# Attention, mixture of experts and SoLU on one core: the tokens of six experts turned on TensorE instead of by DMA

## The chip, the cores and the metric

One Trainium2 chip, one of its cores. The metric is the device time of the whole program in microseconds, lower is better. Every execution of a kernel gives one time; a profiled execution also gives the trace that the rows below are cut from.

Engines by the names of the profile: PE is TensorE (PEld its weight loads), DVE VectorE, ACT ScalarE, POOL GpSimd, SP SyncE, which here only issues DMAs.

## The reference, cut to what matters

```python
def reference(...):
    attn_out = _attn_ref(q, k, v, proj)              # hashed attention, 2 x 8 heads, 768 x 64
    x = attn_out.transpose(0, 2, 1, 3).reshape(1536, 512)
    x = _moe_ref(x, w_gate, w_output_gate, w1, w2)
    return _moe2_ref(x, w_in, w_out, g_ln)           # x @ w_in, SoLU, layer norm, @ w_out

def _moe_ref(x, w_gate, w_output_gate, w1, w2):      # w1 is 8 x 512 x 1024, w2 is 8 x 1024 x 512
    e_idx = np.argmax(x @ w_gate, axis=1)            # one expert for each token
    ...
    for e in range(8):
        mask = e_idx == e
        h = np.maximum(x[mask] @ w1[e], 0.0)
        ye = h @ w2[e]
        out[mask] = gate_w[mask, None] * eom[mask, e, None] * ye
```

Inputs and output are float32. The kernel works with pairs of f16 numbers, a high and a low part, and adds three f16 products for one float32 product.

## The kernel before

Three parts follow each other: attention (to about 264 us), the experts (264 to 416), and the SoLU layer (416 to the end). During attention every token's row, 512 high and 512 low f16 numbers, is scattered by POOL into a table `xs` in DRAM, where each expert has its own rows. The experts are then taken in an order that is computed on the chip from the counts, experts 0 and 1 first and the others by their counts, with a fixed number of columns for each place in the order: 224, 224, 224, 212, 200, 192, 184, 168.

An expert's work is two steps of four slots each. A slot of `m1` is 24 products (two blocks of 128 hidden units, four blocks of the 512 inputs, three f16 products each), with the tokens as the moving operand: `mm1` at lines 1107 to 1109, reading weights `wa` and tokens `xw`. A slot of `m2` is 24 products too: `mm2` at lines 1138 to 1140, reading `wb` and the hidden units `hh`. The list `slots` (lines 1163 to 1167) sets the order, 64 slots in all: m1 of 0, m1 of 1, and then m2 of e and m1 of e + 2 in turn, with m2 of 6 and 7 at the end. So m1 of expert 2 is slots 12 to 15, behind m2 of expert 0 in slots 8 to 11.

Products go to PSUM pool `ps_a`, four tiles of one bank. One slot of m1 fills one tile; ACT reads it twice (`ev1`, lines 1115 and 1117). Two slots of m2 fill one tile; ACT writes its high part to `yT` (`ev2`, L1147) and DVE the low part (L1148). L1148 is put into a list `late` and emitted in the next slot, behind that slot's other DVE work. Pool `ps_h`, two tiles of two banks, is not used in this part.

The weights come as float32 and are split on the way. For each piece of 128 x 1024 numbers, SP loads it into one of five `raw` buffers (`w_load`, L156 for w1, L158 for w2), ACT makes the high part (`w_hi`, L142), and DVE the low part one slot later (`w_lo`, L146), which frees the buffer. The list `prep` gives each slot from 4 to 47 and 52 to 55 one piece, loaded three slots ahead. Between them the SoLU weights are prepared too; they come as 64-bit numbers and need four DVE instructions and two of ACT (`wide_a`, `wide_b`, lines 122 to 131) before their own high and low parts. All this stands in the one loop over `slots` (from line 1209), and each engine works off its share in that order: in a slot ACT has its high part of a weight piece first and the evictions of the slot last.

The tokens: `x_load` (line 1035) takes the 224 rows of an expert out of `xs` by a transposing DMA into `xw`, 128 partitions by 8 blocks by 224 columns, with three buffers. SP issues it in the third slot of m1 of the expert two places earlier. Expert 0 has its tokens from another way.

Of the kernel before, what the change touches and what calls it, by code (L numbers as in the profile page):

```python
# [9 lines left out]
F16 = mybir.dt.float16  # L10
# [11 lines left out]
def kernel(  # L22
# [15 lines left out]
    nc = tc.nc  # L38
    B, H, S, D = q.shape
    NBIT = proj.shape[1]  # L40
    NT, DM = out.shape
    E, _, FF = w1.shape
# [5 lines left out]
    KD = DM // 128  # L48
    KF = FF // 128

    CAP = 224
# [16 lines left out]
    xs = dram.tile([E * NT, 2 * DM], F16, name="xs")  # L68
# [3 lines left out]
    ident16 = const.tile([128, 128], F16, name="ident16")  # L72
# [79 lines left out]
    def w_load(name, e, c):  # L152
        t = raw.tile([128, 1024], F32, tag="raw", name="raw")
        es = bass.ds(ids[e], 1) if e in ids else slice(e, e + 1)
        if name == "w1":
            nc.sync.dma_start(out=t, in_=w1[es, c * 128:(c + 1) * 128, :].rearrange("e p f -> (e p) f"))  # L156
        elif name == "w2":
            nc.sync.dma_start(out=t.rearrange("p (f d) -> p f d", f=2),  # L158
                              in_=w2[es, c * 256:(c + 1) * 256, :].rearrange("e (f p) d -> p (e f) d", p=128))
        elif name == "wi":  # L160
            nc.sync.dma_start(out=t, in_=w_in[c * 128:(c + 1) * 128, :])
        else:
            nc.sync.dma_start(out=t.rearrange("p (f d) -> p f d", f=2),
                              in_=w_out[c * 256:(c + 1) * 256, :].rearrange("(f p) d -> p f d", p=128))
        rawq[name, e, c] = t
# [760 lines left out]
    with tc.manual_schedule():  # L926
        with ExitStack() as es:
# [12 lines left out]
            for i in range(NU):  # L940
# [5 lines left out]
                jj, c = divmod(i - 8, 6)  # L946
# [78 lines left out]
        ps_h = ctx.enter_context(tc.tile_pool(name="ps_h", bufs=2, space=PSUM, reuse_waits="tile"))  # L1025

        moe = ExitStack()
        mp = moe.enter_context(tc.tile_pool(name="mp", bufs=2, reuse_waits="tile"))
# [1 line left out]
        for nm in ("wi", "wo"):  # L1030
            wt[nm, 0] = yp.tile([128, 2, 4096], F16, name=nm)
        yT = yp.tile([128, 2, KD, NT + CAP], F16, name="yT")
        xw_t, hh_t = {}, {}

        def x_load(e, r0, w=CAP):
            xw = mp.tile([128, 2 * KD, CAP], F16, tag="xw", name="xw", bufs=3)
            x = nc.sync.dma_start_transpose(out=xw[:, :, 0:w], in_=xs[r0, :])
            xw_t[e] = xw
            if e in (1, "x"):
                for y in scattered:  # L1040
                    tc.add_manual_dep(x.ins, y.name, mybir.DependencyInfo(
                        mybir.DependencyClass.Sync, mybir.DependencyReason.DATA), reason="rows of xs")

        def window():

            d = nc.vector
            nf, sf, done = (exp_f[:, x] for x in range(3))
            f, win_f = (mp.tile([1, x, y], F32, tag=nm, name=nm, bufs=1) for x, y, nm in ((8, E, "wf"), (1, 3, "wg")))
            m = mp.tile([1, 1], F32, tag="wm", name="wm", bufs=1)
            d.tensor_tensor(out=f[:, 0], in0=nf, in1=done, op=ALU.is_gt)  # L1050
            d.scalar_tensor_tensor(out=f[:, 0], in0=iota8[0:1], scalar=1.0, in1=f[:, 0], op0=ALU.add, op1=ALU.mult)
            d.tensor_reduce(out=m, in_=f[:, 0], op=ALU.max, axis=AX.X)
            d.tensor_tensor(out=f[:, 0], in0=f[:, 0], in1=m.to_broadcast([1, E]), op=ALU.is_equal)
            d.tensor_scalar(out=f[:, 1], in0=nf, scalar1=-float(WIN), scalar2=None, op0=ALU.add)
            d.tensor_tensor(out=f[:, 1], in0=f[:, 1], in1=done, op=ALU.min)
            d.tensor_tensor(out=f[:, 2], in0=f[:, 1], in1=row0[0:1], op=ALU.add)
            d.tensor_tensor(out=f[:, 3], in0=f[:, 1], in1=sf, op=ALU.add)
            d.tensor_copy(out=f[:, 4], in_=iota8[0:1])
            d.tensor_tensor(out=f[:, 5:8], in0=f[:, 2:5], in1=f[:, 0:1].to_broadcast([1, 3, E]), op=ALU.mult)
            d.tensor_reduce(out=win_f[:, 0], in_=f[:, 5:8], op=ALU.add, axis=AX.X)  # L1060
            d.tensor_copy(out=win[:, 0:3], in_=win_f[:, 0])
            d.scalar_tensor_tensor(out=done, in0=f[:, 0], scalar=float(WIN), in1=done, op0=ALU.mult, op1=ALU.add)
# [49 lines left out]
        def ev1(e, g, ps, n):  # L1112
            hh, ps = hh_t[e][..., 0:n], ps[..., 0:n]
            o = hh[:, 0, 2 * g:2 * g + 2]
            nc.scalar.activation(out=o, in_=ps, func=AF.Relu, scale=1.0 / 1024.0)
            hf = mp.tile([128, 2, CAP], F32, tag="hf", name="hf")[..., 0:n]
            nc.scalar.activation(out=hf, in_=ps, func=AF.Relu, scale=1.0 / 1024.0)  # L1117
            late.append(lambda: nc.gpsimd.tensor_tensor(out=hh[:, 1, 2 * g:2 * g + 2], in0=hf, in1=o,  # L1118
                                                        op=ALU.subtract))
# [4 lines left out]
        def run_late():  # L1124
            for f in late:
                f()
            late.clear()
# [14 lines left out]
        def ev2(e, g, start, n):  # L1142
            if g % 2 == 0:
                return
            hi, lo = (yT[:, a, g - 1:g + 1, bass.ds(start, n)] for a in range(2))
            py = psy[e][..., 0:n]
            nc.scalar.activation(out=hi, in_=py, func=AF.Copy, scale=1.0 / 1024.0)  # L1147
            late.append(lambda: nc.vector.scalar_tensor_tensor(out=lo, in0=py, scalar=1.0 / 1024.0, in1=hi,  # L1148
                                                               op0=ALU.mult, op1=ALU.subtract))
# [5 lines left out]
        def expert(e):  # L1155
            ids[e], rows[e] = (nc.values_load(slot_i[0:1, x, e:e + 1], engines=[ET.SP], min_val=0, max_val=mx,
                                              skip_runtime_bounds_check_because=why)
                               for x, mx in ((0, E - 1), (1, (E - 1) * NT)))
# [8 lines left out]
        slots = [(kd, e, g) for kd, e in seq for g in range(4)]  # L1167
# [6 lines left out]
        prep += [None] * 4 + [("w2", E - 1, c) for c in range(4)]  # L1174
        prep += [None] * (len(slots) - len(prep))

        LA = 3
        todo = {}
        placed = []

        def put(i, f, *a):
            todo.setdefault(i, []).append((f, a))

        def each(f, pc):
            for a in w_args(*pc):
                f(*a)
# [3 lines left out]
        for x in range(16):  # L1190
            i = WD[x] if wide else 3 + 3 * x
# [7 lines left out]
            elif x % 2 == 0:  # L1199
# [3 lines left out]
                put(i + 1, each, w_lo, pc)  # L1203
        for x in range(4, 4 + LA):
            if prep[x]:
# [3 lines left out]
        for i, (kd, e, g) in enumerate(slots):  # L1209
            if prep[i]:  # L1210
                each(w_hi, prep[i])
            if i and prep[i - 1]:
                each(w_lo, prep[i - 1])
            if 4 <= i < len(prep) - LA and prep[i + LA]:
                w_load(*prep[i + LA])
            if g == 1 and kd == "m1" and e + 3 < E:
                expert(e + 3)
            if g == 2 and kd == "m1" and e + 2 < E:
                x_load(e + 2, bass.ds(rows[e + 2], CAP))
            for f, a in todo.pop(i, []):  # L1220
                f(*a)
            run_late()
            if kd == "m1":
                ev1(e, g, mm1(e, g, CAPS[e]), CAPS[e])
            else:
                mm2(e, g, CAPS[e])
                ev2(e, g, starts[e], CAPS[e])
            if kd == "m2" and 4 * e + g < NTILE:
                t = 4 * e + g
                po = pos_all[:, t:t + 1]  # L1230
                nc.gpsimd.tensor_scalar(out=po, in0=slot_f[:, t:t + 1], scalar1=1.0, scalar2=1.0,
                                        op0=ALU.mult, op1=ALU.mult)
                x = nc.gpsimd.indirect_dma_start(
                    out=meta[:, :], out_offset=bass.IndirectOffsetOnAxis(ap=po, axis=0),
                    in_=me[:, t], in_offset=None).ins
                for y in placed:
                    tc.declare_no_dep(x, y, reason="every token has a row of its own")
                placed.append(x)
            if i == 30:
                mr = mp.tile([128, NTILE, 2], F32, tag="mr", name="mr", bufs=1)  # L1240
                nc.sync.dma_start(out=mr, in_=meta.rearrange("(t p) c -> p t c", p=128))
            if i == 36:
                nc.vector.tensor_copy(out=tok, in_=mr[:, :, 1])
                nc.vector.tensor_scalar(out=csc, in0=mr[:, :, 0], scalar1=float(2.0 ** -22), scalar2=None,
                                        op0=ALU.mult)
# [4 lines left out]
        mp = ctx.enter_context(tc.tile_pool(name="mq", bufs=2, reuse_waits="tile"))  # L1250
# [135 lines left out]
```

## Time and profile before

| | before |
|---|---|
| median of three runs | 554.01 us (552.87 to 557.27) |
| profiled execution, its own time | 556.92 us |
| span of that execution, first to last instruction | 555.1 us |
| mean granted clock of TensorE | 0.985 |
| busy share of PE, DVE, ACT, POOL | 93%, 71%, 62%, 46% |
| bytes moved by DMA | 83.13 MB, 150 GB/s on the mean |

Times in the rows are microseconds from the start of the span. A line such as L1107 is the line of the kernel that issued the instruction; `a<-xw,wa` are the tile written and the tiles read. An engine's idle time before an instruction stands in brackets with what ended it.

### The profile page before, as it was taken

The page shows a single profiled execution, that of the slowest core. Times are in us where ns is not written, and L with a number is a line of the kernel's source. Part 1 is how long each engine was busy: PE and PEld are TensorE (multiplying, and loading weights), DVE is VectorE, ACT ScalarE, POOL GpSimd, SP SyncE. Part 2 cuts the span into 40 slices and gives each one's busy share as a digit, 9 for nine tenths or more (in the row PEclk, how much of TensorE's full clock was granted, in tenths as well). Part 3 has the DMA queues.
Part 4 walks back from the last instruction along what each step waited for, and adds up shares of the span by engine and source line. Part 5 has one row for each costly group of instructions (what it writes and reads, how often), then busy time and mean ns, then how long its engine had stood idle before and what let it go on. Part 6 is the DMA issues. An engine that isn't in the chain of part 4 may idle for free. (4 is left out here: it accounts for less than half of the span.)

```text
span 555.1 us, 10812 instructions
## 1 busy us (share of the span) xinstructions
PE 518.3 (93%) x3900; PEld 351.5 (63%) x3900; DVE 395.9 (71%) x893; ACT 342.0 (62%) x642; POOL 257.7 (46%) x324
## 2 busy tenths in 40 slices
PE   6789999999999999999997989988999899999993
PEld 5446566666656655667996979987994344444441
DVE  7757777777777787766799987689995875645620
ACT  6677777877867777863386766587643453433420
POOL 7949493939696764716147546232220011121122
PEclk9999999999999999999998989998999999999998
DMA  5584977654839244304777999999600244243271
GB/s 170 109 222 105 225 151 221 151 155 103 230 82 222 90 92 132 91 1 170 234 219 144 330 225 262 235 341 342 243 3 2 43 85 100 58 89 83 57 113 58
DMA packets 107177, 83.13 MB, mean 150 GB/s; under 512 B 80624, under 2 KB 89456, under 8 KB 107120
## 3 DMA queue, kind: packets, MB, share of 16 engines
q1 hardware_dynamic: 104816, 76.09, 53.3%
q0 software_dynamic: 2304, 6.31, 3.2%
q8 instruction: 32, 0.52, 0.4%
q14 instruction: 25, 0.20, 0.1%
HBM read 51.43 MB, written 9.97 MB: 111 GB/s over the span
## 5 line engine op out<-in xcount | busy, mean ns | idle before, releaser
L566 ACT ACTIVATE p<-s,mx 128x768 f32<-128x768 f32 x96 | 95.2, 992 | 51.1 <-DVE mx L555 42.1
L551 DVE TENSOR_REDUCE mx<-s 128x1 f32<-128x768 f32 x96 | 91.7, 955 | 47.9 <-PE s L541 45.9
L580 PE MATMUL t<-ident,p 128*128 128x128 f32 x576 | 124.9, 274 | 0.7 <-ACT pt L582 0.7
L582 ACT COPY pt<-t 128x384 f32<-128x384 f32 x192 | 84.6, 478 | 10.8 <-PE t L580 9.5
L580 PEld LDWEIGHTS t<-ident,p 128*128 128x128 f32 x576 | 77.8, 141 | 15.3 <-ACT pt L582 5.0
L599 PE MATMUL v<-pt,v 128*64 128x384 f32 (+1 forms) x384 | 80.1, 503 | 0.9 <-DVE xt L626 0.9
L1118 POOL TENSOR_TENSOR hh<-hf,hh 128x448 f16<-128x448 f32 (+5 forms) x32 | 40.2, 1259 | 80.1 <-ACT hf L1117 80.1
L1262 PE MATMUL h<-wi,yT 128*128 128x512 f16 x288 | 65.8, 386 | 4.2 <-DVE so L1288 2.6
L1107 PE MATMUL a<-xw,wa 128*128 128x224 f16 (+5 forms) x224 | 57.3, 259 | 9.8 <-DVE yT L1148 8.8
L1138 PE MATMUL a<-hh,wb 128*128 128x224 f16 (+5 forms) x256 | 63.7, 252 | 0.0
L1139 PE MATMUL a<-hh,wb 128*128 128x224 f16 (+5 forms) x256 | 63.6, 251 | 0.0
L1140 PE MATMUL a<-hh,wb 128*128 128x224 f16 (+5 forms) x256 | 63.5, 251 | 0.0
L1329 PE MATMUL o<-wo,zT 128*128 128x512 f16 x288 | 63.5, 379 | 0.0
L541 PE MATMUL s<-k,q 128*128 128x384 f16 x192 | 58.3, 330 | 4.1 <-ACT p L566 4.1
L541 PE MATMUL s<-b,cm 128*128 128x384 f16 x192 | 57.2, 326 | 2.3 <-DVE b L510 1.1
L1109 PE MATMUL a<-xw,wa 128*128 128x224 f16 (+5 forms) x224 | 57.5, 260 | 1.4 <-DVE wa L146 1.4
L1108 PE MATMUL a<-xw,wa 128*128 128x224 f16 (+5 forms) x224 | 57.4, 259 | 0.0
L1262 PEld LDWEIGHTS <-yT 128*128 128x128 f16 x288 | 28.2, 99 | 40.3 <-DVE so L1288 3.8
L1329 PEld LDWEIGHTS <-zT 128*128 128x128 f16 x288 | 28.2, 98 | 34.0
L541 PEld LDWEIGHTS <-q 128*128 128x128 f16 x192 | 19.0, 99 | 39.7 <-issue 37.7
L1277 ACT ACTIVATE ex<-h,st,csc 128x1024 f32<-128x1024 f32 x12 | 14.4, 1203 | 43.3 <-DVE st L1300 32.6
L1301 POOL TENSOR_TENSOR st<-st,nhalf 128x2 f32<-128x2 f32 x12 | 8.5, 707 | 68.6 <-DVE st L1300 68.6
(255 smaller groups left out, 1017.7 us busy)
## 6 DMA issues: line engine op xcount, KB each, us to landing
raw<-in_moe_w_dram SPq DMA_DIRECT2D x64, 512.0 KB, 5.8
raww<-in_moe_w_in_dram SPq DMA_DIRECT2D x8, 512.0 KB
raww<-in_moe_w_out_dram SPq DMA_DIRECT2D x8, 512.0 KB, 6.9
xs<-raw SPq DMA_DIRECT2D x8, 448.0 KB
v<-in_v_dram SPq DMA_DIRECT2D x8, 384.0 KB
q<-in_q_dram SPq DMA_DIRECT2D x7, 384.0 KB, 3.8
k<-in_k_dram SPq DMA_DIRECT2D x7, 384.0 KB, 5.5
cm<-q SPq DMA_DIRECT2D x14, 96.0 KB, 2.1
```

The source lines that it names most:

```text
L541: nc.tensor.matmul(t[:, c, 0:SB], d[x, h][:, s], flat(d[y, h])[:, c * SB:(c + 1) * SB], start=first, stop=not first)
L551: nc.vector.tensor_reduce(out=mx[:, 0:1], in_=t[:, :, 0:SB], op=ALU.max, axis=AX.XY)
L566: nc.scalar.activation(out=p, in_=s_t.pop(i)[:, :, 0:SB], func=AF.Exp, scale=mx[:, 1:2], bias=mx[:, 2:3], accum_out=sums[j][:, qt, h:h + 1])
L580: nc.tensor.transpose(t[:, g * 128:(g + 1) * 128], p[:, c, g * 128:(g + 1) * 128], ident)
L582: nc.scalar.copy(out=pt[j, h][:, 3 * c:3 * c + 3, qt * 128:(qt + 1) * 128], in_=t[:, 0:SB].rearrange("p (g c) -> p g c", g=3))
L599: nc.tensor.matmul(pv[j, q0][64 * h:64 * h + 64, 0:w], vt[:, h, c], pt[j, h][:, c, q0 * 128:q1 * 128], start=(c == 0), stop=(c == NS - 1), ...
L1109: nc.tensor.matmul(ps[:, i, 0:n], w[:, 1, kk, fs], xw[:, kk], start=False, stop=(kk == KD - 1))
L1138: nc.tensor.matmul(ps, w[:, 0, f, ds], hh[:, 0, f], start=(f == 0), stop=False)
L1139: nc.tensor.matmul(ps, w[:, 0, f, ds], hh[:, 1, f], start=False, stop=False)
L1140: nc.tensor.matmul(ps, w[:, 1, f, ds], hh[:, 0, f], start=False, stop=(f == KF - 1))
L1262: nc.tensor.matmul(ps[:, c], yT[:, a, kk, ts], w_i[:, w, kk, c * 512:(c + 1) * 512], start=(kk == 0 and a == 0 and w == 0), stop=(kk == KD ...
L1329: nc.tensor.matmul(ps, zT[:, KF * a + f], w_o[:, w, f], start=(f == 0 and a == 0 and w == 0), stop=(f == KF - 1 and a == 1))
```

## The change

`x_load` keeps the transposing DMA for expert 1 and for the loop on overflowing tokens (`"x"`), which is not entered for these inputs. For experts 2 to 7 it loads rows: 112 partitions, two rows of 1024 f16 numbers on each, into a new tile `xr` with two buffers. A new function `x_turn` makes `xw` out of it: 16 transposes on TensorE (two halves of 512 inputs, four blocks of 128, two groups of 112 rows) into two tiles of `ps_h`, and two copies on ACT from PSUM into `xw`, which now has two buffers. `x_turn` is called in the slot before m1 of the expert, behind `run_late()` and ahead of that slot's own products.

```diff
         def x_load(e, r0, w=CAP):
-            xw = mp.tile([128, 2 * KD, CAP], F16, tag="xw", name="xw", bufs=3)
-            x = nc.sync.dma_start_transpose(out=xw[:, :, 0:w], in_=xs[r0, :])
-            xw_t[e] = xw
+            if e in (1, "x"):
+                xw = mp.tile([128, 2 * KD, CAP], F16, tag="xw", name="xw")
+                x = nc.sync.dma_start_transpose(out=xw[:, :, 0:w], in_=xs[r0, :])
+                xw_t[e] = xw
+            else:
+                xr = mp.tile([CAP // 2, 2, 2 * DM], F16, tag="xr", name="xr")
+                nc.sync.dma_start(out=xr, in_=xs[r0, :].rearrange("(r p) c -> p r c", r=2))
+                xr_t[e] = xr
...
+        def x_turn(e):
+
+            xr = xr_t.pop(e)
+            n = CAP // 2
+            xw = xw_t[e] = mp.tile([128, 2 * KD, CAP], F16, tag="xw", name="xw")
+            ps = [ps_h.tile([128, 2, 1024], F16, tag="h", name="xp")[:, 0] for b in range(2)]
+            for b in range(2):
+                for c in range(KD):
+                    for r in range(2):
+                        nc.tensor.transpose(ps[b][:, c * CAP + r * n:c * CAP + (r + 1) * n],
+                                            xr[:, r, (b * KD + c) * 128:(b * KD + c + 1) * 128], ident16[0:n, 0:n])
+            for b in range(2):
+                nc.scalar.copy(out=xw[:, b * KD:(b + 1) * KD], in_=ps[b][:, 0:KD * CAP].rearrange("p (c n) -> p c n", c=KD))
...
+        xr_at = [("m1", e, 0) for e in range(2, E)]
...
             run_late()
+            if i + 1 < len(slots) and slots[i + 1] in xr_at:
+                x_turn(slots[i + 1][1])
             if kd == "m1":
```

Lines behind `x_load` stand 19 or more lower in the changed kernel: L1107 becomes L1126, L1147 becomes L1166.

On ACT, in slots 10 and 11 (the third and fourth of m2 of expert 0), the order before is this, `wi` being a SoLU weight and `yT` the evictions of m2:

```order
L1147 ACTIVATE yT<-a 128x2x224 [waits PE_49]
L142 ACTIVATE wa<-raw 128x1024 [waits DMAHW7_49]
L142 ACTIVATE wi<-db 128x512 [waits DVE_49]
L142 ACTIVATE wa<-raw 128x1024 [waits DMAHW0_49]
L1147 ISA
L1147 ACTIVATE yT<-a 128x2x224 [waits PE_49]
```

and of the changed kernel, at the same place:

```order
L1166 ACTIVATE yT<-a 128x2x224 [waits PE_49]
L142 ACTIVATE wa<-raw 128x1024 [waits DMAHW7_49]
L142 ACTIVATE wi<-db 128x512 [waits DVE_49]
L142 ACTIVATE wa<-raw 128x1024 [waits DMAHW0_49]
L1061 COPY xw<-xp 128x896 [waits PE_49] x2
L1166 ISA
L1166 ACTIVATE yT<-a 128x2x224 [waits PE_49]
```

The two copies stand behind both weight conversions of the slots and ahead of the second eviction.

On PE, where m1 of expert 2 begins (behind the last product of slot 11), the order before:

```order
L1140 MATMUL a<-hh,wb 128x224
L1107 LDWEIGHTS wa [waits DMAHW2_49,PE_49]
L1107 MATMUL a<-xw,wa 128x224 [waits Activation_49]
L1108 LDWEIGHTS wa
L1108 MATMUL a<-xw,wa 128x224
```

and of the changed kernel:

```order
L1159 MATMUL a<-hh,wb 128x224
L1126 LDWEIGHTS wa
L1126 MATMUL a<-xw,wa 128x224 [waits Activation_49]
L1127 LDWEIGHTS wa
L1127 MATMUL a<-xw,wa 128x224 [waits Activation_49]
```

The wait for the transposing DMA is gone, and the second product waits for ACT as well: the first needs the first half of `xw`, the second the other. The 16 transposes stand 24 products earlier, at the head of slot 11, and the first of them waits for the row load.

On SP, where the tokens of expert 6 are loaded, the order before:

```order
L156 DMA raw<-in_moe_w_dram 128x1024 [waits DMAHW6_49,DVE_49]
L1037 ISA
L1037 DMA_TRANSPOSE xw<-xs 128x8x224 [waits DMAHW4_49,PE_49]
L1241 DMA mr<-meta 128x12x2 [waits DMASW7_49,Pool_49]
L156 ISA
```

and of the changed kernel:

```order
L156 DMA raw<-in_moe_w_dram 128x1024 [waits DMAHW6_49,DVE_49]
L1042 ISA
L1042 DMA xr<-xs 112x2x1024 [waits DMAHW4_49,PE_49]
L1263 DMA mr<-meta 128x12x2 [waits DMASW7_49]
L156 ISA
```

The row load stands where the transposing load stood.

## Rows read from the trace of the kernel before

**Rows 1.** The page: TensorE's busy time, and its clock in 40 slices.

```profile
PE 518.3 (93%) x3900; PEld 351.5 (63%) x3900; DVE 395.9 (71%) x893; ACT 342.0 (62%) x642; POOL 257.7 (46%) x324
...
PEclk9999999999999999999998989998999999999998
```

**Rows 2.** Busy time by stretch: PE, PEld, DVE, ACT, POOL, PEclk, DMA share, GB/s.

```profile
283.60:292.80 9.20, 9.20 (x99) 9.20 (x97) 9.13 (x9) 6.74 (x12) 4.63 (x4) 1.00 0.58 166
292.80:307.60 14.80, 11.28 (x99) 10.03 (x97) 14.73 (x17) 9.36 (x14) 9.90 (x11) 0.88 0.78 166
...
316.80:329.00 12.20, 10.07 (x98) 9.56 (x96) 9.90 (x13) 7.82 (x12) 6.45 (x7) 0.89 1.04 249
329.00:347.30 18.30, 18.07 (x195) 17.75 (x194) 14.65 (x15) 13.38 (x21) 11.00 (x13) 0.98 0.98 246
347.30:356.00 8.70, 8.70 (x99) 8.70 (x97) 6.60 (x5) 5.49 (x9) 3.28 (x3) 1.00 1.06 222
356.00:365.90 9.90, 8.10 (x99) 7.95 (x97) 5.89 (x9) 4.69 (x8) 0.22 (x1) 1.00 0.95 329
365.90:374.10 8.20, 8.20 (x99) 8.20 (x96) 7.80 (x9) 6.92 (x12) 4.68 (x4) 1.00 1.14 308
374.10:386.10 12.00, 9.48 (x99) 9.14 (x98) 11.93 (x14) 10.07 (x17) 2.88 (x3) 0.86 0.93 346
...
394.00:415.70 21.70, 21.69 (x291) 21.48 (x288) 20.36 (x28) 11.80 (x22) 5.01 (x4) 1.00 0.23 85
```

**Rows 3.** Waits of PE, 285 to 420 us: total, times, longest.

```profile
PE a L1107 <- DVE yT L1148: 8.8, 5, 2.5
```

**Rows 4.** Timeline of ACT in the expert part: start, duration, instruction, idle before.

```profile
299.55 0.63 ACT L142 ACTIVATE wi<-db 128x512 f16<-128x512 f32 x1 [1.76 <-DVE db L131]
...
301.03 0.53 ACT L1147 ACTIVATE yT<-a 128x448 f32 x1
...
318.87 0.53 ACT L1147 ACTIVATE yT<-a 128x448 f32 x1
...
338.06 1.06 ACT L142 ACTIVATE wa<-raw 128x1024 f16<-128x1024 f32 x1 [2.87 <-DMA raw<-in_moe_w_dram]
...
341.53 0.53 ACT L1147 ACTIVATE yT<-a 128x448 f32 x1
...
359.28 1.06 ACT L142 ACTIVATE wa<-raw 128x1024 f16<-128x1024 f32 x1 [3.23 <-DMA raw<-in_moe_w_dram]
...
361.97 0.50 ACT L1147 ACTIVATE yT<-a 128x424 f32 x1
...
380.71 0.48 ACT L1147 ACTIVATE yT<-a 128x400 f32 x1
...
396.92 0.48 ACT L1147 ACTIVATE yT<-a 128x384 f32 x1
```

**Rows 5.** Timeline of DVE near 360 us.

```profile
360.37 1.23 DVE L146 SCALAR_TENSOR_TENSOR wa<-raw,wa 128x1024 f16<-128x1024 f32 x1 [2.62 <-ACT wa L142]
```

**Rows 6.** SP: all transposing token loads (ns min/median/max), and its timeline from 347 us.

```profile
L1037 SPq DMA_TRANSPOSE xw<-xs x7: 1487/4407/5222, 265.9 to 366.6; - x7
...
347.60 4.41 SPq L1037 DMA_TRANSPOSE xw<-xs  x1
...
353.65 3.21 SPq L156 DMA_DIRECT2D raw<-in_moe_w_dram  x2
```

**Rows 7.** Stretches that DMA spent on a transposing load, and on weight rows.

```profile
312.00:314.00 2.00, 2.00 (x24) 2.00 (x22) 2.00 (x2) 1.51 (x3) 1.35 (x2) 1.00 1.26 246
338.00:340.00 2.00, 2.00 (x26) 2.00 (x24) 0.65 (x2) 1.74 (x2) 1.68 (x3) 1.00 1.03 410
```

**Rows 8.** f16 transposes on PE near the start: one group, and the durations in ns.

```profile
10.70 0.50 PE L378 MATMUL tp<-ident,kl 128*128 128x128 f16 x6
...
L378 PE MATMUL tp<-ident,kl x12: 219/219/243, 5.8 to 11.0; 128*64 128x128 f16 x6, 128*128 128x128 f16 x6
```

**Rows 9.** The nearest copy on ACT: f16 from PSUM, 768 columns.

```profile
L463 ACT COPY k<-tp x1: 805/805/805, 10.0 to 10.0; 128x768 f16<-128x768 f16 x1
```

More of the change, by code (lines that the diff above doesn't have):

```diff
@@ L1032 @@
         yT = yp.tile([128, 2, KD, NT + CAP], F16, name="yT")
-        xw_t, hh_t = {}, {}
+        xw_t, xr_t, hh_t = {}, {}, {}
         def x_load(e, r0, w=CAP):
-            xw = mp.tile([128, 2 * KD, CAP], F16, tag="xw", name="xw", bufs=3)
-            x = nc.sync.dma_start_transpose(out=xw[:, :, 0:w], in_=xs[r0, :])
-            xw_t[e] = xw
+            if e in (1, "x"):
[6 more added lines that the diff above has]
+                xr_t[e] = xr
             if e in (1, "x"):
```

## The prediction

> **What bounds the kernel now.** I began with the page: TensorE is busy for 93% of the span [rows 1], but the page says of a busy PE that it is not PE at its peak, so the question is where its instructions are spaced out. The change touches the expert stage alone. The view of busy time by stretch, cut at borders of slots, tells it [rows 2]. Four slots of 24 products with 224 columns take 9.2 us when nothing is late (283.6 to 292.8). The same work in 292.8 to 307.6 takes 14.8, so 5.6 us are lost there; 307.6 to 316.8 is again 9.2. With 212 columns four slots are 8.7 us, with 200 columns 8.2, so with 192 and 184 columns, in proportion, 7.9 and 7.6. By these, 316.8 to 329.0 loses 12.2 - 8.7 = 3.5 us, 329.0 to 347.3 loses 18.3 - 9.2 - 8.2 = 0.9, 356.0 to 365.9 loses 2.0 and 374.1 to 386.1 loses 4.4. After 307.6 that makes **10.8 us**, and nothing is lost after 394.
>
> The waits name the cause: PE at L1107 waits 8.8 us in 5 places for L1148 on VectorE [rows 3], the eviction that frees a PSUM tile of pool a. A second part is the clock: its mean is 0.88 in the 14.8 us from 292.8 [rows 2], that is some 3.5 us at 1.2 instead of 2.4 GHz behind such a wait, worth 1.7 us of work.
>
> Why L1148 is late stands in the timelines of ACT and DVE. Both prepare weights in program order, slot by slot, and run *behind* PE: in slot 11 (the fourth of m2 of expert 0) ACT first waits 1.76 us for DVE and gets to its last eviction at 301.03 [rows 4], though PE began the next slot at 292.8 [rows 2]. PE's four PSUM tiles let it run up to four slots ahead; that lead is what it uses up. After 320 the preparers are late again for another reason: ACT waits 2.87 and 3.23 us for weights from DMA [rows 4], and DVE then 2.62 for ACT [rows 5]. Ahead of the 3.23 stands a transposing load on SP at 347.60 that holds the queue 4.41 us; the next weight loads go out at 353.65 [rows 6].
>
> **The change, part by part.**
>
> *SP and DMA.* Six of the seven transposing loads become row loads. One transposing load holds SP 1.5 to 5.2 us, median 4.4; two weight loads beside it take 3.21 together with their waits, so at most 1.6 each [rows 6]. A weight load behind it thus goes out up to 4 us earlier. On the DMA engines, a stretch filled by a transposing load moves 246 GB/s, a stretch of weight rows 410 [rows 7]: for 448 KB that is 1.9 against 1.1 us, a gain of 0.8 us an expert. The Trainium skill says otherwise (Advanced Engine Details and Errata, § X-Bar Transpose (TRN2)): there transposing DMAs on this chip are as fast as regular ones. By that rule the DMA engines would gain nothing; rows 7 disagree on the rate, and the rule is silent on SP's time.
>
> *PE.* 16 small transposes are added in the slot before each of experts 2 to 7. The trace has a like row: six f16 transposes 128x128 in 0.50 us, one of them 0.22 long, so (0.50 - 0.22)/5 = 0.056 us each [rows 8]. 16 of them are 0.9 us (0.8 if 112 columns scale it down). The first set lies inside a stall (below), five are paid: **+4.5 us**.
>
> *ACT.* Two copies 128x896 from PSUM to f16 per expert. 128x768 takes 0.805 us [rows 9]; 896 columns scale to 0.94, and two in a row, overlapping a little, are 1.75. ACT is busy 9.36 of 14.8 us there [rows 2], so this is covered as work. It is not covered as a *place*: the copies stand in ACT's order behind the weight conversions of that slot, and the first product of the next expert on PE now waits for them. Queued behind PE's wait are all products of that expert; behind ACT's copies, the second eviction of the slot. Before, the tokens came by DMA, and no product needed ACT to be up to date so soon.
>
> *First border, m1 of expert 2.* ACT reaches the place of the copies at 301.03 [rows 4], and nothing before it changes: ACT waits there for DVE, and DVE is busy 9.13 of the 9.20 us before 292.8 and 14.73 of the 14.80 after it [rows 2]. So m1(2) starts at 301.03 + 1.75 = 302.8 instead of 292.8. Its four slots then run with all PSUM tiles free, but after a gap of 10 us I charge one drop of the clock (1.7): 302.8 + 9.2 + 1.7 = 313.7, against 307.6. **+6.1 us.**
>
> *From there on* PE is late enough that, if it never waits again, the starts are: m1(3) 313.7 + 9.2 + 0.9 = 323.8; m1(4) + 8.7 + 9.2 + 0.9 = 342.6; m1(5) + 8.2 + 8.7 + 0.9 = 360.4; m1(6) + 7.9 + 8.2 + 0.9 = 377.4; m1(7) + 7.6 + 7.9 + 0.9 = 393.8; end + 21.7 = 415.5, against 415.7. That is 6.1 + 4.5 - 10.8 = **-0.2 us**: the lead that PE had is spent in one piece at the first border, not in five.
>
> *The borders behind it.* PE now needs ACT up to date at each. Where ACT stood before, plus 1.75, is 320.6, 343.3, 363.7, 382.5 and 398.7 [rows 4]; against the starts above it is 3.2 early, then 0.7, 3.3, 5.1 and 4.9 late. If the preparers gain nothing, the largest of these, 5.1 us, is added. If each border gets back what it waited for behind a transposing load (2.87 of ACT for m1(4), 3.23 for m1(5) [rows 4], 2.62 of DVE for the last two [rows 5]), at most 2.5 is left, and 0 if the shorter waits around them go too. I take **1.5**, nearer to the low end, since the long waits are the ones that the removed loads head.
>
> What lies behind the stage (h, softmax, output) begins when PE ends it and only shifts. The sum on the profiled execution is 556.9 - 0.2 + 1.5 = 558.2 us (span 555.1 and 1.8 around it). That execution stands 2.9 above the median of the three runs, 554.0; on the median the same +1.3 gives **555.3 us**. The ends of the border term, 0 and 5.1, with one more drop of the clock at the upper, give 553.8 and 560.6.
>
> **The rivals.**
>
> 1. *The preparers gain nothing*: weight loads land as late as before because DMA is nearly full either way (share 0.95 to 1.14 in 347 to 374 [rows 2]). Then -0.2 + 5.1 = +4.9, and with a wait over 2 us and its drop of the clock +6.6: 558.9 to 560.6. For it speaks that DVE has no free time in 374 to 386 (11.93 of 12.00 [rows 2]). Against it, the two long ACT waits that follow transposing loads.
>
> 2. *Faster*: the first border costs nothing. This needs ACT to reach the copies by 291, ten us sooner than it did; then -0.2 - 6.1 = -6.3: 547.7. The place from which it decides is the conversion at 299.55 that waits for DVE [rows 4]; I see nothing in the change that speeds DVE up before it.
>
> 3. *The clock does not take transposes for work.* The 2.0 us lost in 356.0 to 365.9 left the clock at 1.00, the losses of 3.5 us and more did not [rows 2]; 0.9 us of transposes beside a wait of a us or so would then act as one longer gap at each of five borders, 1.7 us each: +1.3 + 8.5, 563.8. The Trainium skill has this rule (TensorE: Matmul & The Clock Gate, § Part 4: PE-mode transpose): transposes do not count as busy in the same way. The trace does not bear it out: through the attention part, where the transposes of L580 alternate with products, the clock row of the page shows full tenths [rows 1].
>
> 4. *The change does not do what it says*: the row loads come so late that the transposes wait. Each is issued 12 slots ahead of its use, some 25 us; I give it nothing of its own.
>
> **How the numbers follow.** Forecast as summed, 0.62; rival 1, 0.21; rival 2, 0.11; rival 3, 0.06. A measurement of this kernel can tell about 1% from no change, which is 5.5 us. Slower by more than that are half of rival 1, all of rival 3 and a tail of 0.04 of the forecast (two late weight loads at borders, each with its drop of the clock): 0.21. Faster is rival 2: 0.11. The rest, 0.68, is within 1%. The range leaves out the far half of rival 2 below and the far tail above: 550.5 to 562.5; the likeliest case alone spans 553.8 to 558.9.
>
> **What would show it.** Right: a gap on PE of about 10 us before m1 of expert 2 that ends on ACT's copy; after it m1(2) without waits for L1148; small waits for the copy, under 2 us, before m1(4) to m1(7); L1148 gone or nearly gone from PE's waits; SP's row loads under 1.6 us; the stage ending within 2 us of 415.7. Wrong: ACT at the copies by 295 (rival 2); waits of 3 us and more for the copy before m1(5) and m1(6) (rival 1); clock at its lower level after short waits (rival 3).

## The result, and the profile after

The changed kernel takes 560.5 us (median of 6 runs, 557.7 to 562.5) against 553.8 us (6 runs, 551.9 to 557.3): a ratio of **1.0127, 95% interval 1.0098 to 1.0156**, slower by about 1.3%. The forecast was 555.3 us, with a range of 550.5 to 562.5, and most of the chance on a difference within 1%. The time lies in the range, 5.2 us above the forecast, and the difference is over the 1% within which most of the chance lay.

The two profiled executions differ by less, 561.3 against 556.9 us: the expert stage begins 0.5 us later, is 5.1 us longer (264.5 to 421.3, 156.8 us, against 264.0 to 415.7, 151.7), and what lies behind it is 1.2 us shorter. The medians differ by more, 6.7 us, since the profiled execution before stands 3.1 us above its median and the changed one 0.8. What a profile can show is therefore the 5 us in the stage.

The page of the changed kernel, for [rows 1]: the clock row now has a 6 where there were an 8 and 9s.

```profile
PE 521.8 (93%) x3996; PEld 355.9 (64%) x3996; DVE 393.5 (70%) x893; ACT 353.4 (63%) x654; POOL 259.3 (46%) x324
...
PEclk9999999999999999999996999998999989999998
```

Busy time by stretch, changed kernel, for [rows 2]; the borders are now the first products of m1 of experts 2 (302.46), 3 (324.31), 4 (343.93), 5 (362.40), 6 (380.81) and 7 (399.50), and at 294.06 and 314.31 the ends of m2 of 0 and m1 of 2. Columns as there.

```profile
294.06:302.46 8.40, 0.15 (x3) 0.00 (x1) 8.33 (x12) 5.93 (x9) 6.71 (x8) 0.68 0.67 157
302.46:314.31 11.85, 11.39 (x96) 10.36 (x96) 8.42 (x10) 8.36 (x13) 3.06 (x3) 0.80 1.00 268
314.31:324.31 10.00, 10.00 (x115) 10.00 (x114) 9.22 (x9) 7.54 (x10) 8.84 (x8) 1.00 0.88 272
324.31:343.93 19.62, 18.87 (x211) 18.71 (x208) 16.74 (x17) 15.15 (x23) 14.58 (x15) 1.00 0.91 293
343.93:362.40 18.47, 17.91 (x209) 17.76 (x209) 13.57 (x14) 15.23 (x22) 4.08 (x4) 1.00 0.87 255
362.40:380.81 18.41, 17.11 (x210) 16.96 (x209) 17.33 (x21) 15.38 (x24) 5.04 (x4) 1.00 0.97 322
380.81:399.50 18.69, 18.12 (x208) 17.94 (x208) 14.64 (x19) 12.89 (x21) 4.56 (x4) 0.91 0.83 300
```

PE is idle for 8.3 us before m1 of expert 2 and runs at a mean clock of 0.80 behind that gap; later it loses 0.75 us before m1 of 4 (324 to 344), 0.56 inside it, 1.30 before m1 of 6, 0.57 inside it, and the mean clock is 0.91 from there to m1 of 7. The drop lies in one stretch, which has half the full clock:

```profile
382.40:385.90 3.50, 3.50 (x27) 3.47 (x25) 3.43 (x6) 1.77 (x4) 0.33 (x1) 0.51 0.84 291
```

PE's waits from 262 to 424 us (total, times, longest), for [rows 3]. The five waits for L1148 are gone; in their place stand waits for ACT's copy, L1061.

```profile
PE a L1126 <- ACT xw L1061: 10.3, 3, 8.3
PE a L1127 <- ACT xw L1061: 1.6, 3, 0.6
```

The timeline of ACT, changed kernel, for [rows 4]: the first border, and the border of m1 of expert 6 with what follows it.

```profile
300.04 0.63 ACT L142 ACTIVATE wi<-db 128x512 f16<-128x512 f32 x1 [1.76 <-DVE db L131]
...
301.52 1.69 ACT L1061 COPY xw<-xp 128x896 f16<-128x896 f16 x2
...
379.25 0.72 ACT L142 ACTIVATE wo<-db,g 128x512 f16<-128x512 f32 x1 [1.80 <-DVE db L131]
379.88 1.69 ACT L1061 COPY xw<-xp 128x896 f16<-128x896 f16 x2
...
384.64 0.48 ACT L1134 ACTIVATE hh<-a 128x368 f16<-128x368 f32 x1 [1.73 <-PE a L1128]
...
394.95 0.50 ACT L1166 ACTIVATE yT<-a 128x384 f32 x1 [2.16 <-PE a L1159]
```

The timeline of PE at the first border, m1 of expert 4 and m1 of expert 6, changed kernel, and below it the kernel before at m1 of expert 6.

```profile
302.46 0.35 PE L1126 MATMUL a<-xw,wa 128*128 128x224 f16 x1 [8.25 <-ACT xw L1061]
...
343.93 0.25 PE L1126 MATMUL a<-xw,wa 128*128 128x200 f16 x1 [0.75 <-ACT xw L1061]
...
380.81 0.24 PE L1126 MATMUL a<-xw,wa 128*128 128x184 f16 x1 [1.30 <-ACT xw L1061]
```

```profile
374.10 0.24 PE L1107 MATMUL a<-xw,wa 128*128 128x184 f16 x1
```

This pair is the core of the case. At m1 of expert 6 ACT stands nearly where it stood before: its copies begin at 379.88, and the eviction at the same place of the order began at 380.71 in [rows 4]. But before, PE had begun m1 of expert 6 at 374.10, 6.6 us ahead of ACT, and now it may begin only at 380.81, behind the first copy.

All waits of ACT from 308 to 416 us show the other half. Before, the first fence, ACT waits for DMA and for DVE, never for PE. After, the second fence, it hardly waits for DMA, less for DVE, and 17.3 us for PE's products (9.4 + 7.9).

```profile
ACT wo L142 <- DVE db L131: 16.8, 7, 3.7
ACT wb L142 <- DMA raw<-in_moe_w_dram: 10.7, 7, 3.2
ACT wa L142 <- DMA raw<-in_moe_w_dram: 7.7, 6, 3.2
```

```profile
ACT yT L1166 <- PE a L1159: 9.4, 8, 2.2
ACT hh L1134 <- PE a L1128: 7.9, 13, 3.0
ACT wo L142 <- DVE db L131: 6.1, 4, 2.9
ACT wa L142 <- DMA raw<-in_moe_w_dram: 2.5, 5, 1.1
```

So PE waits for ACT at a border, and ACT, done with the copies, then waits for PE to make something to evict.

SP, changed kernel, for [rows 6]: the row loads hold SP for 0.33 us each, and the pair of weight loads that went out at 353.65 now goes out at 350.18.

```profile
L1042 SPq DMA_DIRECT2D xr<-xs x6: 333/334/349, 273.6 to 365.9; - x6
```

```profile
350.18 3.74 SPq L156 DMA_DIRECT2D raw<-in_moe_w_dram  x2
```

The added work, changed kernel: a copy's duration (ns, min/median/max), for [rows 9], and the stretch that one set of 16 transposes takes on PE, for [rows 8].

```profile
L1061 ACT COPY xw<-xp x12: 886/906/911, 301.5 to 398.1; 128x896 f16<-128x896 f16 x12
```

```profile
290.95:291.74 0.79, 0.79 (x18) 0.79 (x17) 0.79 (x2) 0.79 (x3) 0.06 (x1) 1.00 0.80 270
```

### The profile page after: what moved, and what is told of

The parts are those of the page before. It is cut to its first block, busy times and chain, and to the rows that moved or that the text cites. A ratio compares the mean times of both kernels' runs of the same rounds, so it can differ in the third digit from the quotient of the medians.

```text
span 559.5 us, 11014 instructions
## 1 busy us (share of the span) xinstructions
PE 521.8 (93%) x3996; PEld 355.9 (64%) x3996; DVE 393.5 (70%) x893; ACT 353.4 (63%) x654; POOL 259.3 (46%) x324
## 5 line engine op out<-in xcount | busy, mean ns | idle before, releaser
L1126 PE MATMUL a<-xw,wa 128*128 128x224 f16 (+5 forms) x224 | 57.0, 258 | 11.3 <-ACT xw L1061 10.3
```

The lines of the kernel that those rows point to most:

```text
L1126: nc.tensor.matmul(ps[:, i, 0:n], w[:, 0, kk, fs], xw[:, kk], start=(kk == 0), stop=False)
```

## The experiments

Two questions: is it the added work, or the place of the copies in ACT's order; and if the place, which border? All ratios are to runs of the kernel before made beside the experiment (its medians there 556.5 to 556.7), each with its 95% interval.

**No wait for the copies.** All work stays, but no product needs it. The products of experts 2 to 7 read expert 1's tokens, which are given a buffer of their own so that they stay; the main line of the edit:

```diff
-            xw = xw_t[e][:, :, 0:n]
+            xw = xw_t[e if e in (0, "x") else 1][:, :, 0:n]
```

> The changed kernel, but the products of experts 2 to 7 read expert 1's tokens, which lie there since before the stage; the transposes and the copies are still made, and nothing reads the copies. Place theory (the loss is that PE waits for copies that stand late in ACT's order): the gap of 8.3 us before m1 of expert 2 and the waits of 1.3 and 1.9 us before m1 of experts 4 and 6 go, PE uses up its lead at L1148 again, and the time is 548 to 556 us, a ratio of 0.99 to 1.005. Work theory (the loss is the work that is added, 0.8 us of transposes on PE and 1.75 us of copies on ACT for each expert): the ratio stays at 1.010 to 1.013.

Measured: ratio 1.0007 (0.9982 to 1.0032). The largest row of PE's waits in it, 275 to 424 us:

```profile
PE a L1126 <- DVE yT L1167: 7.6, 4, 3.1
```

The lead is used up at the late eviction again, as in [rows 3], and the loss is gone although the work is there. The place theory holds.

**No token loads at all.** The kernel before without its six transposing loads; experts 2 to 7 read expert 1's tokens by the same line as above, and `xw` has two buffers:

```diff
-            if g == 2 and kd == "m1" and e + 2 < E:
+            if g == 2 and kd == "m1" and e + 2 < 2:
```

> The kernel before without its six transposing loads of the expert stage, and without anything in their place: the products of experts 2 to 7 read expert 1's tokens. It tells what taking the transposing loads off SP and DMA is worth at most. If they head the late weight loads, PE's losses of 10.8 us after 307 fall below half, and the time is 546 to 549 us, a ratio of 0.985 to 0.993. If the preparers are bound by VectorE's and ACT's own work, the ratio is 0.996 to 1.000.

Measured: ratio 0.9924 (0.9879 to 0.9970), inside the first range. But the reason given for it does not hold: PE waits for L1148 no less than before (10.4 us, against 8.8 in [rows 3]). That row, and ACT's waits from 308 to 416 us:

```profile
PE a L1107 <- DVE yT L1148: 10.4, 5, 4.1
...
ACT wo L142 <- DVE db L131: 13.8, 6, 3.8
ACT wa L142 <- DMA raw<-in_moe_w_dram: 8.7, 4, 4.0
ACT wb L142 <- DMA raw<-in_moe_w_dram: 6.6, 7, 1.6
```

15.3 us for weight pieces, against 18.4 before: without any token load the weights still come late. The long waits for DMA were not, in the main, headed by the transposing loads. All six loads together are worth 0.8%, and the profiled execution does not show where: its stage is 152.2 us long, as before. It took 557.8 us, the slowest of five (median 553.8), so its waits may be longer than usual.

**Four and six slots ahead.** The same work, turned earlier (six: the same with 6):

```diff
-            if i + 1 < len(slots) and slots[i + 1] in xr_at:
-                x_turn(slots[i + 1][1])
+            if i + 4 < len(slots) and slots[i + 4] in xr_at:
+                x_turn(slots[i + 4][1])
```

> The changed kernel with transposes and copies placed four slots ahead of their use, not one. Place theory: ACT makes the copies for expert 2 at about 295.4, m1 of expert 2 starts near 297.2 instead of 302.5, the later borders have no wait for a copy, and the ratio is 0.997 to 1.006. Work theory: the same work at another place, 1.010 to 1.013.

> The changed kernel with transposes and copies placed six slots ahead of their use. Place theory: the copies for expert 2 are done by about 287, no border has a wait for a copy, what is gained by the row loads shows, and the ratio is 0.985 to 1.000. Work theory: 1.010 to 1.013.

Measured: 0.9975 (0.9948 to 1.0002) with four, 0.9941 (0.9917 to 0.9966) with six. Only the place differs from the changed kernel, and that is worth 1.5 to 1.9%. With four, m1 of expert 2 began at 296.72, near the 297.2 expected, and of the later borders only m1 of 3 still had a wait, 0.56 us. With six, no border waits for a copy, but the copies for expert 2 began at 291.23, not by 287: there is a new wait before the first border, on PE, since the row load of expert 2 has not landed when its transposes want it.

```profile
PE xp L1058 <- DMA xr<-xs: 4.7, 1, 4.7
```

**Which border?** The prediction had charged 6.1 us to the first one, and its rival 2 counted on getting them back. If that were where the time goes, taking the first wait away should bring it back. Three kernels: expert 2 keeps its transposing load and 3 to 7 are turned one slot ahead (from 3); experts 4 to 7 are turned six slots ahead and 2, 3 one (late 6); and the mirror image (early 6). The first hunk is from 3's, whose list of turned experts also begins at 3; the second is late 6's, and early 6 has the 1 and the 6 exchanged.

```diff
-            if e in (1, "x"):
+            if e in (1, 2, "x"):
...
-            if i + 1 < len(slots) and slots[i + 1] in xr_at:
-                x_turn(slots[i + 1][1])
+            for d, es in ((1, (2, 3)), (6, (4, 5, 6, 7))):
+                if i + d < len(slots) and slots[i + d] in xr_at and slots[i + d][1] in es:
+                    x_turn(slots[i + d][1])
```

> The changed kernel, but expert 2 keeps its transposing load too; turned are experts 3 to 7, one slot ahead as before. The wait of 8.3 us before m1 of expert 2 goes. First-gap theory (that gap is what the time is lost in): a new wait of about 3 us before m1 of expert 3 and a ratio of 1.003 to 1.007. Last-border theory (PE catches up with the preparers late in the stage in every kernel, and what counts is that from a late border on it can't run ahead of them; what is won early is waited for again at m1 of experts 4 and 6): m1 of expert 6 starts as late as in the changed kernel, near 381, and the ratio stays at 1.010 to 1.013.

> The changed kernel with experts 4 to 7 turned six slots ahead, and 2 and 3 one slot ahead as in the change. The gap before m1 of expert 2 stays (about 8 us), the waits before m1 of 4 and 6 go. First-gap theory: at least half of the loss stays, ratio 1.005 to 1.010. Last-border theory: the loss is gone, m1 of expert 6 starts near 376 and PE uses up its lead in it, ratio 0.994 to 1.001.

> The mirror image: experts 2 and 3 turned six slots ahead, 4 to 7 one slot ahead. First-gap theory: half or more of the loss is gone, 1.000 to 1.005. Last-border theory: m1 of expert 6 waits for ACT as in the changed kernel, ratio 1.009 to 1.013.

Measured: from 3, 1.0157 (1.0098 to 1.0216); late 6, 1.0001 (0.9973 to 1.0030); early 6, 1.0131 (1.0079 to 1.0183). All three go against the first-gap theory and with the last-border theory, though not in every figure: from 3 lies above its range (the interval reaches it), and in late 6 m1 of expert 6 began at 379.13, not near 376, and PE never used up its lead in it. PE's waits for the copy in from 3 (308 to 416 us), its stretch of the same time, and then the first wait and that stretch of late 6:

```profile
PE a L1126 <- ACT xw L1061: 7.8, 4, 4.1
PE a L1127 <- ACT xw L1061: 2.6, 5, 0.6
```

```profile
308.00:416.00 108.00, 97.57 (x1146) 95.77 (x1144) 90.36 (x97) 79.83 (x123) 41.42 (x38) 0.98 0.81 251
```

```profile
303.12 0.35 PE L1126 MATMUL a<-xw,wa 128*128 128x224 f16 x1 [8.22 <-ACT xw L1061]
```

```profile
308.00:416.00 108.00, 108.00 (x1294) 107.68 (x1292) 90.97 (x103) 83.57 (x130) 43.44 (x40) 0.99 0.80 253
```

Late 6 has the whole gap of 8.2 us at the first border and is no slower than before: from 308 on PE is never idle. From 3 has no gap there and then waits 10.4 us at five borders. In early 6 the wait moves on as well: 4.7 us before m1 of expert 4, 1.30 before m1 of 6.

The starts below are read from PE's timeline, in us from the first product of the stage:

| kernel | ratio | m1 of 6 begins | m2 of 5 begins | stage ends |
|---|---|---|---|---|
| before | 1 | 110.1 | 122.1 | 151.7 |
| changed (all one slot ahead) | 1.0127 | 116.3 | 126.3 | 156.8 |
| from 3 | 1.0157 | 118.9 | 127.2 | 158.2 |
| early 6 | 1.0131 | 119.8 | 128.1 | 159.0 |
| all two ahead | 1.0069 | 114.8 | 122.4 | 152.7 |
| late 6 | 1.0001 | 114.0 | 122.4 | 152.0 |
| no wait for copies | 1.0007 | 111.6 | 121.9 | 152.6 |
| all four ahead | 0.9975 | 111.3 | 122.1 | 151.7 |

Weight pieces are prepared in every slot up to 47, the last of m1 of expert 6, and only four more behind it. What seems to count is when PE is through slot 47, that is the column of m2 of 5. The kernels that do not wait for a copy at m1 of 6 get there at 122, wherever they have waited before; the three that do are at 126 to 128. The table has one profiled execution of each kernel, and the ratios many runs. Two slots ahead does not fit: its execution is through slot 47 at 122.4, as late 6 is, and yet its runs are 0.7% slower than before. The kernels that are not in the table are there at 119.0 to 122.7, with ratios from 0.992 to 1.001 that the column does not order. What late 6 and early 6 do show is that the loss belongs to the borders of experts 4 to 7; which of these four it is was not separated, and that the border at m1 of 6 is the last that counts because the pieces end there is argued, since the number of pieces was not varied.

**Two slots ahead.**

> The changed kernel with transposes and copies two slots ahead of their use. One slot ahead gave 1.013, four 0.9975, six 0.994. If the wait for ACT's place shrinks with each slot of distance (one slot is 1.9 to 2.3 us of PE), the ratio is 1.004 to 1.010; if what counts is only whether the copies stand ahead of the slot's own late conversions, two slots are as good as four, 0.996 to 1.001.

Measured: 1.0069 (1.0031 to 1.0106), the first of the two. Where the loss lies is open: the profiled execution, 557.2 us where the median is 559.5, waits 7.30 us at m1 of 2 and 1.02 at m1 of 4, and not at m1 of 6. One slot costs 1.3%, two 0.7%, four and six nothing that can be told: the first three slots of distance buy 1.5%, 8.4 us, the next ones little that can be told. That the bend lies at four, as many as PE has PSUM tiles to run ahead in, fits; with another number of tiles it was not tried.

**A faster kernel?** Expert 2 with its transposing load and the others six slots ahead; expert 2 four slots and the others six; all six ahead once more; and all six ahead with expert 2's row load put ahead of the stage's first weight loads, and left out at its old place:

```diff
+        x_load(2, bass.ds(rows[2], CAP))
         for x in range(4, 4 + LA):
             if prep[x]:
                 w_load(*prep[x])
...
-            if g == 2 and kd == "m1" and e + 2 < E:
+            if g == 2 and kd == "m1" and 2 < e + 2 < E:
```

> A version meant to beat both: expert 2 keeps its transposing load (turned six slots ahead, its row load came 4.7 us late for the transposes in the profiled execution), experts 3 to 7 are turned six slots ahead. Place theory: no wait for a row load and none for a copy, a ratio of 0.988 to 0.996. If late row loads of expert 2 cost nothing over many runs, the ratio is that of all six turned six slots ahead, 0.994.

> A version meant to beat both: expert 2 turned four slots ahead (its row load was 4.7 us late for a turn six slots ahead), experts 3 to 7 six slots ahead. If the late row load costs the median run something, the ratio is 0.988 to 0.993; by the last-border theory a gap so early in the stage is won back later, and the ratio stays at 0.993 to 0.997.

> The version with all six turned six slots ahead, once more and in more rounds: 0.992 to 0.997 if its 0.994 holds; 1.000 if that was the chip's scatter, as the version that keeps expert 2's transposing load (1.0012) may hint.

> All six turned six slots ahead, and the row load of expert 2 moved on SP's queue ahead of the first five weight loads of the stage, right behind expert 1's transposing load. The wait of 4.7 us before the first transposes goes. If it costs, 0.985 to 0.992; if a gap so early is won back later, 0.992 to 0.997.

Measured: 1.0012 (0.9985 to 1.0039), 0.9961 (0.9929 to 0.9993), 0.9984 (0.9960 to 1.0008) and 0.9965 (0.9938 to 0.9992). The first missed what was expected of it, and why it is no faster stays open: its profiled stage, 151.2 us, has no wait for a copy. The repeat of six ahead gives 0.9984 where it gave 0.9941, outside the range that was expected if the 0.9941 held; the intervals just overlap. Early loading removes the wait for the rows but gains nothing that can be told from the others, which fits that wait too being won back. Expert 2 at four slots has the shortest profiled stage of all, 148.7 us. What can be said is that all six experts turned four slots and more ahead gave ratios 0.2 to 0.6% under 1 in five measurements, in three of them with an interval that leaves out 1. Row loads with transposes on PE are thus a small gain at most, once they are far enough ahead.

## Why the prediction was right, and where it was wrong

**The first border: right in place, short in price.** m1(2) was to start at 302.8 and starts at 302.46, behind ACT's copy; its four slots were to end at 313.7 and end at 314.31. The clock cost more than the 1.7 us charged: 11.85 us less 9.2 of work and the 0.46 of the second wait leaves 2.2.

**PE and ACT: right.** A set of transposes takes 0.79 us (0.9 charged), two copies 1.69 (1.75).

**The recovered waits: right.** L1148 is gone from PE's waits. The sum of these terms, under the condition that PE never waits again, was -0.2 us. Late 6 is that condition made real, and its stage is 0.3 us longer than before's (152.0 against 151.7).

**The later borders: the step that failed.** The text took 1.5 us, "nearer to the low end, since the long waits are the ones that the removed loads head". It measured 5.2. Against the text's own starts, PE is 1.3 us late at m1(4) (343.93 for 342.6), 2.0 at m1(5) (362.40 for 360.4), 3.4 at m1(6) (380.81 for 377.4) and 5.7 at m1(7) (399.50 for 393.8); the stage ends at 421.3 for 415.5. The 0.6 of the first border taken off, the term is 5.2 us: waits for the copy of 3.2 (0.75, 0.56, 1.30 and 0.57), 1.7 of the clock behind the last two, and some 0.3 spread over the rest. The 1.5 had no drop of the clock in it.

The 5.2 is close to the text's upper bound, 5.1, and the 560.5 us measured fall within the sum of rival 1, 558.9 to 560.6. That is in part luck. Rival 1 had one long wait, 5.1 us at m1(6), on preparers that gain nothing, with a drop of the clock at its upper end. Measured are four short waits that come to 3.2, and the drop; and the 560.5 is a median 6.7 us above the other, where the two executions that were traced differ by 4.4.

The reason given for the low end holds in part only. ACT's copies began 1.4 us sooner than the eviction that stood there before at m1(5) (360.59 for 361.97), and 0.8 sooner at m1(6) (379.88 for 380.71), where the text had hoped for 3.2 and 2.6; at m1(4) they began 1.5 later (342.99 for 341.53), where it had hoped for 2.9. Two readings speak against its cause: without any token load ACT still waits 15.3 us for weight pieces, and of ACT's 18.4 us of waits for them before, 15.9 went in the changed kernel, for which ACT then waited 17.3 for PE. So rival 1's "gain nothing" is not what came either. Nor is its reason, DMA nearly full, what the trace shows: in the changed kernel ACT waits 2.5 us for `wa` pieces, where it waited 7.7.

**What the sum saw, and rival 2 did not.** The sum set the 6.1 us of the first border against the 10.8 of later losses, and late 6 bears that out: it keeps the gap and loses nothing. But the two hang together. Rival 2 took the gap away, kept the 10.8 as a gain, and came to 547.7; from 3 takes it away and is 1.6% slower than before, since PE then waits for copies at five borders. In these kernels PE and its preparers meet again before the end in any case, so a wait early in the stage is paid from time that would be lost later. The term that decided was the small one at the later borders.

**The signs.** Of the signs of the forecast these came: the gap before m1(2) that ends on ACT's copy (8.25 us), no wait for L1148, waits under 2 us before m1(4) to m1(7), row loads of 0.33 us on SP. One did not: the stage ends 5.6 us behind 415.7. Rival 1's sign, waits of 3 us and more before m1(5) and m1(6), did not come (none and 1.30). Rival 3's sign came once.

**The other rivals.** *Faster* did not come: ACT was at the copies at 301.52, not by 291. Rival 3 had the clock fall at each of the later borders. The trace is mixed: the granted clock stays at 1.00 through the waits at m1(4) (0.75 + 0.56 us), and is 0.51, near the lower of its two levels (1.2 of 2.4 GHz), from 382.40 to 385.90, behind 1.30 + 0.57 us at m1(6). That costs 1.7 us, which the sum had only at the upper end of its border term. The Trainium skill (TensorE: Matmul & The Clock Gate, § Part 4: PE-mode transpose) says that a transpose does not count as busy in the same way; one fall behind six sets of transposes neither shows nor excludes it. With the transposes four slots ahead the clock row of the page is full through the whole stage, though PE waits 2.6 us for a copy and up to 2.8 for an eviction in it (its waits from 275 to 424 us, then the row):

```profile
PE a L1126 <- DVE yT L1167: 6.1, 5, 2.8
PE a L1126 <- ACT xw L1061: 2.6, 1, 2.6
```

```profile
PEclk9999999999999999999999999999999999999998
```

The row loads were late for nothing in the changed kernel (rival 4); they were for transposes six slots ahead.

**The chances.** Slower by over 1%, which is what came, had 0.21, half of it from rival 1. The text had numbers for every border, and chose the low value on the order of two rows (a transposing load, then a late weight piece), which no run had tested.

## What to carry to other kernels

When work that an engine gets "for free" is put between two engines, ask not only whether its time is covered but how far the consumer was running ahead of that place: an in-order engine whose result the next product needs immediately cancels the lead that PSUM buffers had given. Put such work as many steps ahead as the consumer ran ahead (here four slots were enough, two were not). And in a stage where two sides alternate in waiting, price a stall at the later places where they meet; an early one may cost nothing at all (here 8.2 us cost nothing), which one run with only the late half of the edit undone will show.

## What the hardware showed unexpectedly

- The clock does not follow one gap by itself: it fell behind 1.87 us of waits at m1(6) of the changed kernel and did not fall behind waits of 2.6 and 2.8 us with the transposes four slots ahead, where it stayed at 1.00 through the stage. What else PE did there was not separated.
- Taking away six transposing loads of 448 KB, which hold SP for some 4 us each [rows 6] and move at 246 GB/s where weight rows move at 410 [rows 7], is worth only 0.8% of the kernel. The Trainium skill (Advanced Engine Details and Errata, § X-Bar Transpose (TRN2)) has transposing DMAs as fast as regular ones; by the rate they are not, by what they cost here the difference is small.
